# First chunk of a pre-LN attention and gMLP kernel: q's first four slices in two column halves, and an opening ordered by hand

## The chip, the cores and the metric

The kernel runs on one core of one Trainium2 chip. The metric is the device time in microseconds of one execution. A profile of one execution comes with the runs. TensorE is PE in the profile (its weight loads PEld), VectorE is DVE, ScalarE is ACT, GpSimd is POOL, and SP is the engine whose queue issues most DMAs.

## The reference

Input x has 2048 rows (tokens) of 1024 columns, in bfloat16. Two blocks follow each other, each behind a layer norm and each added to its input.

```python
x = A_x
h = x + _A_ref(_layernorm(x), A_wqkv, A_wo)
h2 = h + _B_ref(_layernorm(h), B_w_in, B_w_sp, B_b_sp, B_w_out)

# _A_ref: 32 heads of 32; a token looks at itself and at 7 earlier ones, 2 apart
qkv = (x @ wqkv).reshape(B, S, 3, H, Dh)              # wqkv: 1024 x 3072
logits = einsum('bhsd,bhswd->bhsw', q, kg) * scale    # kg: k at s, s-2, ..., s-14
o = einsum('bhsw,bhswd->bhsd', softmax(logits), vg)
return o.reshape(B, S, D) @ wo

# _B_ref: gated MLP with mixing over tokens
z = gelu(x @ w_in)                                    # w_in: 1024 x 3584
z1, z2 = z[..., :1792], layernorm(z[..., 1792:])
g = einsum('ts,bsf->btf', w_sp, z2) + b_sp[None, :, None]
return (z1 * g) @ w_out
```

## The kernel before

Tokens are cut into four chunks of 512 (`CH`), each of four tiles of 128. The matmuls that make q, k and v have a weight slice of 128 columns as the stationary operand (taken with a stride of 8 elements, so that a slice holds one eighth of every group of eight columns) and the transposed, normed tokens `xnT` of one chunk as the moving one, 512 columns wide. There are 8 slices (`dl`) for each of q, k and v, and 8 steps of contraction (`kt`) for each slice. Two slices share a PSUM accumulator of two banks (`new_acc`, three of them in the pool `ps_acc`; a second pool, `ps_att`, has one buffer with the tag `L`).

The kernel has three parts in time. The opening makes `xnT` of chunk 0: for each tile of 128 tokens statistics (`stats` on DVE, L222; `stats_act` on ACT for tile 3, L228), the reciprocal root (`rstd_of`, L237), the norm (`norm`, L242) and eight transposes on PE with a copy out of PSUM (`xpose`, L249). Behind it comes a long middle part, in which the closures of all stages (q, k, v, attention, output projection, the gMLP's first two products) are given to the planner `Order` (L61) with a duration, dependences and a priority each. `Order.run` simulates the engines from given starting clocks and calls the closures in the order of the planned starts; within this part each compute engine then works in exactly that order. Chunks 1 to 3 get their statistics through `ln1` (L290), with arrival times from `X_AT` (L287), go to DRAM normed (`xn_d`) and come back through a transposing DMA on SP's queue. Last comes a dense part: the mixing over tokens (L773) and the last product (L788).

In the opening before, the framework's own scheduler orders the engines' instructions; only `o_.run()` at L751 stands under a schedule kept by hand. q of chunk 0 is part of `qkv` (L329): its first four slices go kt by kt through two accumulators (L338 to L343), since wq arrives in eight pieces, one for each kt; the other slices go one after the other.

SP's queue issues, in this order: tiles 0 and 1 of x (ACT's queue issues 3 and 2), wq in eight pieces, wk, the four tiles of chunk 1, wv, the eight tiles of chunks 2 and 3. Two tiles of x share a buffer (`pairs`), and there are four such buffers, so the tiles of chunk 2 wait until the norms of chunk 0 have read theirs. Ahead of everything PE runs `NWARM` matmuls on zeros (L207).

Of the kernel before, what the change touches and what calls it, by code (L numbers as in the profile page):

```python
# [10 lines left out]
FP32 = mybir.dt.float32  # L11
BF16 = mybir.dt.bfloat16
# [19 lines left out]
NEG = -1.0e9  # L32
NWARM = 14
XRB = 2
# [90 lines left out]
def kernel(  # L125
# [17 lines left out]
    out2d = out[0]  # L143

    consts_d = nc.inline_tensor(_consts(), name="qt_consts")

# [14 lines left out]
    eps_t = cpool.tile([P, 1], FP32, name="eps_t")  # L161
    V.memset(eps_t[:], EPS)
    nhalf = cpool.tile([P, TPC], FP32, name="nhalf")
    V.memset(nhalf[:], -0.5)
    mv1 = cpool.tile([P, NT, 2], FP32, name="mv1")
# [12 lines left out]
    def new_acc():  # L178
        return ps_acc.tile([P, 2, CH], FP32, name="acc", tag="acc")
# [18 lines left out]

    def load_x(i):
        x_slot(i)  # L200
        dma(xts[i], x2d[i * P:(i + 1) * P, :])

# [3 lines left out]
    for _ in range(NWARM):  # L206
        T.matmul(wps[:], warm[:, 0:P], warm[:], start=True, stop=True)  # L207

    for i in (0, 3, 1, 2):
        x_slot(i)  # L210
        (dma if i < 2 else A.dma_start)(xts[i], x2d[i * P:(i + 1) * P, :])
    wsb = [wtile([P, KT, D], "wq", "wA"), wtile([P, KT, D], "wk", "wA"), wtile([P, KT, D], "wv", "wB")]
    for kt in range(KT):
        dma(wsb[0][:, kt, :], wq_view[:, kt, 0:D])
    dma(wsb[1][:], wq_view[:, :, D:2 * D])
    for i in range(TPC, 2 * TPC):
        load_x(i)
    dma(wsb[2][:], wq_view[:, :, 2 * D:3 * D])
    for i in range(2 * TPC, NT):
        load_x(i)  # L220

# [5 lines left out]

    def stats_act(i):  # L228
        sm = l1.tile([P, 4], FP32, name="sm", tag="sm")
        jk = l1.tile([P, D], BF16, name="jk", tag="xn", bufs=4)  # L230
        A.activation(jk[:], xts[i], ACTF.Identity, accum_out=sm[:, 0:1])
        A.activation(jk[:], xts[i], ACTF.Square, accum_out=sm[:, 1:2])
        V.tensor_scalar(mv1[:, i, 0:1], sm[:, 0:1], 1.0 / D, None, op0=ALU.mult)
        V.tensor_tensor(sm[:, 2:3], mv1[:, i, 0:1], mv1[:, i, 0:1], op=ALU.mult)
        V.scalar_tensor_tensor(mv1[:, i, 1:2], sm[:, 1:2], 1.0 / D, sm[:, 2:3], op0=ALU.mult, op1=ALU.subtract)

    def rstd_of(lo, hi):  # L237
        sd = l1.tile([P, TPC], FP32, name="sd1", tag="sd1")
        A.activation(sd[:, 0:hi - lo], mv1[:, lo:hi, 1], ACTF.Sqrt, bias=eps_t[:])
        V.reciprocal(rstd1[:, lo:hi], sd[:, 0:hi - lo])  # L240

# [7 lines left out]
    def xpose(i, xn):  # L249
        tp = ps_acc.tile([P, KT, P], BF16, name="tpa", tag="acc")  # L250
        for a in range(KT):
            T.transpose(tp[:, a, :], xn[:, a * P:(a + 1) * P], ident)  # L252
        (V.tensor_copy if i == 2 else A.copy)(xnT[0][:, :, i * P:(i + 1) * P], tp[:])

    wsq = l1.tile([P, 1], FP32, name="wsq", tag="wsq")
    A.activation(wsq[:], eps_t[:], ACTF.Sqrt)
    stats_act(3)
    stats(V, 0)
    rstd_of(0, 1)
    stats(V, 1)  # L260
    xpose(0, norm(0))
    rstd_of(1, 2)
    rstd_of(3, 4)
    xpose(1, norm(1))
    xpose(3, norm(3))
    stats(V, 2)
    rstd_of(2, 3)
    xpose(2, norm(2))
    wo_sb = wtile([P, DLO, D], "wo_sb", "wB")
# [8 lines left out]

    o_ = Order({"PE": 12.9, "ACT": 12.0, "DVE": 12.6, "POOL": 12.0}, {"acc": 3, "L": 1, "prod": 2, "part": 2, "xn": 4})
    add = o_.add  # L280
# [5 lines left out]

    X_AT = {1: 18.5, 2: 27.5, 3: 30.5}  # L287
    xn_ready = {}
# [25 lines left out]

    att_in = {}

    def alloc_att_in(c):
        qT = att.tile([P, DLO, CH], BF16, name="qT", tag="qT")
        kT = att.tile([P, DLO, HALO + CH], BF16, name="kT", tag="kT")
        vT = att.tile([P, DLO, HALO + CH], BF16, name="vT", tag="vT")  # L320
        att_in[c] = (qT, kT, vT)

    seq = [0]
# [5 lines left out]
    def qkv(c):  # L329
        for xi in range(3):  # L330
            wv = wsb[xi][:].rearrange("p kt (m dl) -> p kt dl m", dl=DLO)
            for dp in range(DLO // 2):
                key = ("acc", "qkv", c, xi, dp)
                deps = [G.get(("xnT", c))]
                if c == 0 and xi == 0 and dp < 2:
                    def mm(wv=wv, dp=dp):
                        if dp == 0:
                            accs = [new_acc(), new_acc()]  # L338
                            G["acc", "qkv", 0, 0, 0], G["acc", "qkv", 0, 0, 1] = accs
                            for kt in range(KT):  # L340
                                for dl in range(4):
                                    T.matmul(accs[dl // 2][:, dl % 2, :], wv[:, kt, dl, :], xnT[0][:, kt, :],  # L342
                                             start=(kt == 0), stop=(kt == KT - 1))  # L343
                    last = add("PE", 6.91 if dp == 0 else 0.0, mm, deps, prio=order(), take="acc")
                else:
                    for j in range(2):
                        def mm(j=j, dl=2 * dp + j, wv=wv, key=key):
                            if j == 0:
                                G[key] = new_acc()
                            for kt in range(KT):  # L350
                                T.matmul(G[key][:, j, :], wv[:, kt, dl, :], xnT[c][:, kt, :],  # L351
                                         start=(kt == 0), stop=(kt == KT - 1))
                        last = add("PE", 1.727, mm, deps, prio=order(), take="acc" if j == 0 else None)
                        deps = [last]
                def ev(xi=xi, dp=dp, key=key):
                    if c == 0:
                        off = 0 if xi == 0 else HALO
                        A.copy(att_in[0][xi][:, 2 * dp:2 * dp + 2, off:off + CH], G[key][:])  # L358
                        if xi > 0 and dp == 3:
                            dma(qkv_d[xi][:, :, CH - HALO:CH], att_in[0][xi][:, :, CH:CH + HALO])  # L360
                    else:
                        stg = l1.tile([P, 2, CH], BF16, name="stg", tag="xn", bufs=4)
                        A.copy(stg[:], G[key][:])  # L363
                        dma(qkv_d[xi][:, 2 * dp:2 * dp + 2, c * CH:(c + 1) * CH], stg[:])
# [9 lines left out]
    def attention(c):  # L374
        if c == 0:
            d_q = G["ev", 0, 0, 3]
            d_k, d_v = G["ev", 0, 1, 3], G["ev", 0, 2, 3]
# [318 lines left out]


    alloc_att_in(0)
    V.memset(att_in[0][1][:, :, 0:HALO], 0.0)
    V.memset(att_in[0][2][:, :, 0:HALO], 0.0)  # L700
    qkv(0)
# [47 lines left out]
    dma_op(0.0, wsp0, [G["z1ev", NCH - 2], G["close"]])  # L749
    with tc.manual_schedule(engines={mybir.EngineType.PE, mybir.EngineType.Activation, mybir.EngineType.DVE, mybir.EngineType.Pool}):  # L750
        o_.run()  # L751
    t2.close()
# [81 lines left out]
```

## Time and profile before

| what | value |
|---|---|
| median of 3 runs | 737.69 us (737.46 to 737.92) |
| time of the profiled execution | 737.65 us |
| its span | 735.9 us |
| mean granted clock of PE | 0.998 of full |
| PE busy | 725.7 us, 99% of the span |
| DVE, ACT, POOL busy | 416.8, 219.2, 50.0 us |
| DMA | 105.27 MB, mean 143 GB/s |

A line of a timeline gives the start in us, the busy time in us, engine, line of the code, operation, and written<-read tiles with shapes and the number of instructions merged into it; in brackets stands the time for which the engine was idle before it, and what ended that. A line of the windows gives the stretch in us, its length, the busy time of PE, PEld, DVE, ACT and POOL (with the number of instructions), the granted clock of PE as a share of full speed, the busy share of the DMA engines and GB/s. A matmul's listed duration (379 ns for 512 columns) is longer than its pitch, since matmuls are pipelined: 224 matmuls of L773 take 48.35 us in the chain, 0.216 us each.

### The profile page before, as it was taken

To read this page: it belongs to the slowest core of one execution; us is meant where nothing else is said; L and a number is where in the kernel's file an instruction comes from. 1 tells how busy PE (TensorE), PEld (TensorE's weight loads), DVE (VectorE), ACT (ScalarE), POOL (GpSimd) and SP (SyncE) were. 2 spreads that over 40 slices of the span, in tenths; PEclk is the share of its full clock that TensorE was granted. 3 is DMA by queue.
4 is the path that set the end of the run, shared out by engine and by line. 5 is a ranking of instruction groups with operands and counts; after the bars stand their busy time and mean duration, and the time that the engine had idled before them with its cause. 6 is when DMAs were issued, how large, how long until landed. Compare 5 with 4: busy or idle time off the path is not lost.

```text
span 735.9 us, 8608 instructions
## 1 busy us (share of the span) xinstructions
PE 725.7 (99%) x3580; PEld 369.1 (50%) x3580; DVE 416.8 (57%) x431; ACT 219.2 (30%) x267; POOL 50.0 (7%) x59
## 2 busy tenths in 40 slices
PE   7999999999999999999999999999999999999998
PEld 4666665566645444444444544444444444444444
DVE  4899899988999899889940012221232223212322
ACT  4322532534338954696563620000000000000000
POOL 0310200100102100300113000000000000000000
PEclk9999999999999999999999999999999999999999
DMA  9874563485484632370079988135104410020002
GB/s 337 315 242 116 191 184 122 153 231 200 149 324 109 210 113 74 115 227 18 29 229 338 256 243 268 40 95 148 58 29 112 133 57 31 28 86 29 1 15 71
DMA packets 113223, 105.27 MB, mean 143 GB/s; under 512 B 67776, under 2 KB 91744, under 8 KB 113056
## 3 DMA queue, kind: packets, MB, share of 16 engines
q1 hardware_dynamic: 105472, 72.63, 33.0%
q0 software_dynamic: 7280, 31.50, 12.1%
q8 instruction: 28, 0.46, 0.3%
q10 hardware_dynamic: 432, 0.59, 0.2%
q14 instruction: 11, 0.09, 0.0%
HBM read 55.09 MB, written 33.88 MB: 121 GB/s over the span
## 4 chain that ended last, share of the span: by engine, by line
PE 89%; DVE 7%; ACT 1%; POOL 1%; issue 1%; DMA 0%; POOLq 0%; DVEq 0%; ACTq 0%
PE acc L773 26%; PE acc L351 22%; PE acc L788 13%; PE acc L627 10%; PE acc L677 9%; PE acc L554 8%; DVE prod L504 2%; DVE oT L510 2%; PE acc L342 1%; DVE part L411 1%; POOL l3rstd L524 1%; PE L L430 1%; DMA xp<-in_A_x_dram 0%; PE tpa L252 0%; ACT z1s L683 0%
## 5 line engine op out<-in xcount | busy, mean ns | idle before, releaser
L773 PE MATMUL acc<-wspT,z2sb 128*128 128x512 bf16 x896 | 194.0, 379 | 0.0
L773 PEld LDWEIGHTS <-z2sb 128*128 128x128 bf16 x896 | 87.7, 98 | 105.7
L776 DVE TENSOR_TENSOR g<-acc,bB 128x1024 bf16<-128x1024 f32 x28 | 34.3, 1224 | 157.6 <-PE acc L773 133.0
L677 PE MATMUL acc<-hnT,win 128*128 128x512 bf16 x448 | 99.4, 379 | 0.5 <-ACT z1s L683 0.5
L627 PE MATMUL acc<-win,hnT 128*128 128x512 bf16 (+1 forms) x512 | 99.3, 352 | 0.0
L627 PEld LDWEIGHTS <-hnT 128*128 128x128 bf16 x512 | 49.8, 98 | 47.7 <-issue 0.9
L407 DVE TENSOR_TENSOR prod<-qT,kT 128x4096 bf16<-128x4096 bf16 x32 | 72.0, 2284 | 1.6 <-ACT kT L358 1.6
L788 PEld LDWEIGHTS <-zg 128*128 128x128 bf16 x462 | 45.2, 98 | 51.7
L677 PEld LDWEIGHTS <-win 128*128 128x128 bf16 x448 | 43.4, 98 | 52.5 <-issue 1.7
L504 DVE TENSOR_TENSOR prod<-vT,AB 128x4096 bf16<-128x4096 bf16 x28 | 63.8, 2289 | 1.0
L510 DVE TENSOR_TENSOR oT<-oT,prod 128x4096 bf16<-128x4096 bf16 x28 | 64.0, 2284 | 0.1
L363 ACT CAST stg<-acc 128x1024 bf16<-128x1024 f32 x36 | 36.4, 1011 | 78.6 <-PE acc L351 75.5
L788 PE MATMUL acc<-wout_a,zg 128*128 128x512 bf16 (+1 forms) x264 | 58.2, 373 | 0.0
L795 DVE TENSOR_TENSOR ot<-acc,hr 128x1024 bf16<-128x1024 f32 x15 | 18.4, 1224 | 69.4 <-PE acc L788 69.4
L351 PE MATMUL acc<-xnT,wv 128*128 128x512 bf16 x256 | 57.1, 380 | 0.0
L351 PE MATMUL acc<-xnT,wk 128*128 128x512 bf16 x256 | 57.1, 380 | 0.0
L554 PE MATMUL acc<-wo_sb,oT 128*128 128x512 bf16 x256 | 56.3, 379 | 0.7 <-DVE oT L510 0.7
L351 PE MATMUL acc<-xnT,wq 128*128 128x512 bf16 x224 | 49.8, 379 | 0.0
L351 PEld LDWEIGHTS <-wk 128*128 128x128 bf16 x256 | 36.4, 143 | 19.1 <-issue 0.9
L351 PEld LDWEIGHTS <-wv 128*128 128x128 bf16 x256 | 36.4, 143 | 19.1 <-issue 0.9
L788 PE MATMUL acc<-wout_b,zg 128*128 128x512 bf16 (+1 forms) x198 | 44.4, 373 | 0.0
L351 PEld LDWEIGHTS <-wq 128*128 128x128 bf16 x224 | 31.9, 143 | 16.8 <-issue 0.8
(125 smaller groups left out, 489.9 us busy)
## 6 DMA issues: line engine op xcount, KB each, us to landing
qkv_d<-stg SPq DMA_DIRECT2D x36, 256.0 KB, 2.5
z_d<-z1s SPq DMA_DIRECT2D x28, 256.0 KB, 2.6
z1c<-z_d SPq DMA_DIRECT2D x28, 256.0 KB, 2.7
z_d<-u SPq DMA_DIRECT2D x12, 448.0 KB, 2.9
z2sb<-z_d POOLq DMA_DIRECT2D x12, 448.0 KB, 9.2
xr<-in_A_x_dram SPq DMA_DIRECT2D x16, 256.0 KB, 2.8
h_d<-hb SPq DMA_DIRECT2D x16, 256.0 KB, 2.4
win<-in_B_w_in_dram POOLq DMA_DIRECT2D x2, 2048.0 KB, 9.1
```

The lines of the kernel that those rows point to most:

```text
L351: T.matmul(G[key][:, j, :], wv[:, kt, dl, :], xnT[c][:, kt, :], start=(kt == 0), stop=(kt == KT - 1))
L363: A.copy(stg[:], G[key][:])
L407: V.tensor_tensor(st["prod"][:], qT[:], kT[:, :, o:o + CH], op=ALU.mult)
L504: V.tensor_tensor(pvs[w][:], vT[:, :, o:o + CH], abb, op=ALU.mult)
L510: prev = add("DVE", 2.3, lambda w=w: V.tensor_tensor(oTs[c][:], oTs[c][:], pvs[w][:], op=ALU.add), [prev, m_], prio=3.0, lat=0.15, free="p ...
L554: T.matmul(st["acc", il][:, nh, :], oTs[c][:, dl, il * P:(il + 1) * P], wo_sb[:, dl, nh * CH:(nh + 1) * CH], start=(dl == 0), stop=(dl == ...
L627: T.matmul(accf[:, n0:n1], hnTs[c][:, il, kt, :], wins[hf][:, kt, n0:n1], start=(kt == 0), stop=(kt == KT - 1))
L677: T.matmul(G["accy", c, fp][:, j, :].rearrange("p (a b) -> p a b", a=TPC), wt[:, kt, f0 * P:(f0 + 1) * P], hnTs[c][:, :, kt, :], start=(kt ...
L773: T.matmul(acc[:, j, :], z2sb[a][:, f * P:(f + 1) * P], wspT[:, a, :], start=(a == 0), stop=(a == NT - 1))
L776: V.tensor_tensor(g1[:], acc[:], bB[:, c * CH:(c + 1) * CH].unsqueeze(1).to_broadcast([P, 2, CH]), op=ALU.add)
L788: T.matmul(outs, zg[:, f, il * P:(il + 1) * P], wt[:, f0, lo:hi], start=(f == 0), stop=(f == NF - 1))
L795: V.tensor_tensor(ot[:], acc[:].rearrange("p a b -> p (a b)"), hr[:], op=ALU.add)
```

## The change

The four compute engines are now ordered by hand from the start of the kernel. The opening is written out in the order that each engine shall keep:

- Tiles 0 and 1 of x are loaded in two halves of 64 partitions each, one on SP's and one on ACT's queue. Chunk 1's x (two loads of two tiles) goes ahead of wk, the first half of what follows ahead of wv.
- Two more matmuls on zeros; the constants' memsets go behind the one that these matmuls wait for.
- `stats_act` is split into two sums, and the second one and its variance come after tiles 0 and 1 have been transposed. Tiles 2 and 3 share one root.
- `xpose` puts its eight transposes into two PSUM banks of one buffer, even tiles in `L`, odd ones in `acc`; `xput` copies one half with ACT and the other with DVE.
- q's first four slices are made with 64 matmuls of 256 columns instead of 32 of 512: the left half, tokens of tiles 0 and 1, with `q_left`, between whose steps the transposes of tiles 2 and 3 stand; then the right half, slice by slice. The other four slices follow as before, all ahead of the planner, which gets later starting clocks and new arrival times.

```diff
-NWARM = 14
+NWARM = 16
...
+    by_hand = tc.manual_schedule(engines={mybir.EngineType.PE, mybir.EngineType.Activation, mybir.EngineType.DVE, mybir.EngineType.Pool})
+    by_hand.__enter__()
...
+    def load_pair(k):
+        x_slot(2 * k)
+        x_slot(2 * k + 1)
+        dma(pairs[k][:], x2d[2 * k * P:(2 * k + 2) * P, :].rearrange("(t p) d -> p t d", p=P))
...
-    for i in (0, 3, 1, 2):
-        x_slot(i)
-        (dma if i < 2 else A.dma_start)(xts[i], x2d[i * P:(i + 1) * P, :])
...
+    with tc.manual_schedule(engines={mybir.EngineType.SP}):
+        for i in range(TPC):
+            x_slot(i)
+        for i in range(2):
+            dma(xts[i][0:64], x2d[i * P:i * P + 64, :])
+            A.dma_start(xts[i][64:P], x2d[i * P + 64:(i + 1) * P, :])
+        dma(xts[2], x2d[2 * P:3 * P, :])
+        A.dma_start(xts[3], x2d[3 * P:4 * P, :])
+        for kt in range(KT):
+            dma(wsb[0][:, kt, :], wq_view[:, kt, 0:D])
+        load_pair(2)
+        load_pair(3)
+        dma(wsb[1][:], wq_view[:, :, D:2 * D])
+        load_pair(4)
+        load_pair(5)
+        dma(wsb[2][:], wq_view[:, :, 2 * D:3 * D])
+        load_pair(6)
+        load_pair(7)
...
     def xpose(i, xn):
-        tp = ps_acc.tile([P, KT, P], BF16, name="tpa", tag="acc")
+        tps[i] = ps_acc.tile([P, 2, 2 * CH], BF16, name="tpb", tag="acc") if i % 2 else ps_att.tile([P, 2, 2 * CH], BF16, name="tpa", tag="L")
         for a in range(KT):
-            T.transpose(tp[:, a, :], xn[:, a * P:(a + 1) * P], ident)
-        (V.tensor_copy if i == 2 else A.copy)(xnT[0][:, :, i * P:(i + 1) * P], tp[:])
+            T.transpose(tps[i][:, a // 4, (a % 4) * P:(a % 4 + 1) * P], xn[:, a * P:(a + 1) * P], ident)
+
+    def xput(i):
+        for hf, cp in ((0, A.copy), (1, V.tensor_copy)):
+            cp(xnT[0][:, 4 * hf:4 * hf + 4, i * P:(i + 1) * P], tps[i][:, hf, 0:CH].rearrange("p (a s) -> p a s", a=4))
+
+    def q_mm(dl, kt, lo, hi):
+        T.matmul(qacc[dl // 2][:, dl % 2, lo:hi], wqs[:, kt, dl, :], xnT[0][:, kt, lo:hi], start=(kt == 0), stop=(kt == KT - 1))
+
+    def q_left(lo, hi):
+        for kt in range(lo, hi):
+            for dl in range(4):
+                q_mm(dl, kt, 0, 256)
+
+    def q_out(dp):
+        A.copy(att_in[0][0][:, 2 * dp:2 * dp + 2, :], qacc[dp][:])
...
-    stats_act(3)
     stats(V, 0)
-    rstd_of(0, 1)
+    sd0 = root(0, 1)
+    sm = sums_act(3, 0)
     stats(V, 1)
-    xpose(0, norm(0))
-    rstd_of(1, 2)
-    rstd_of(3, 4)
-    xpose(1, norm(1))
-    xpose(3, norm(3))
+    sd1 = root(1, 2)
+    V.reciprocal(rstd1[:, 0:1], sd0[:, 0:1])
+    xn = {0: norm(0)}
+    V.reciprocal(rstd1[:, 1:2], sd1[:, 0:1])
+    xn[1] = norm(1)
+    xpose(0, xn[0])
+    xput(0)
+    xpose(1, xn[1])
+    xput(1)
+    qacc[0], qacc[1] = new_acc(), new_acc()
     stats(V, 2)
-    rstd_of(2, 3)
-    xpose(2, norm(2))
+    sums_act(3, 1, sm)
+    var_act(3, sm)
+    sd2 = root(2, 4)
+    V.reciprocal(rstd1[:, 2:4], sd2[:, 0:2])
+    xn[2], xn[3] = norm(2), norm(3)
+    q_left(0, 6)
+    xpose(2, xn[2])
+    xput(2)
+    q_left(6, 7)
+    xpose(3, xn[3])
+    xput(3)
+    q_left(7, KT)
+    for dp in range(2):
+        for dl in (2 * dp, 2 * dp + 1):
+            for kt in range(KT):
+                q_mm(dl, kt, 256, CH)
+        q_out(dp)
+    for dp in (2, 3):
+        qacc[dp] = new_acc()
+        for dl in (2 * dp, 2 * dp + 1):
+            for kt in range(KT):
+                q_mm(dl, kt, 0, CH)
+        q_out(dp)
...
-    o_ = Order({"PE": 12.9, "ACT": 12.0, "DVE": 12.6, "POOL": 12.0}, {"acc": 3, "L": 1, "prod": 2, "part": 2, "xn": 4})
+    o_ = Order({"PE": 24.8, "ACT": 25.8, "DVE": 14.4, "POOL": 12.0}, {"acc": 3, "L": 1, "prod": 2, "part": 2, "xn": 4})
...
-    X_AT = {1: 18.5, 2: 27.5, 3: 30.5}
+    X_AT = {1: 13.0, 2: 20.5, 3: 28.5}
```

In `qkv` the loop over q, k and v starts at k for chunk 0, and in `attention` the dependence of chunk 0 on q is a fixed planned time of 26.0.

## The prediction

> **What bounds the kernel now.** I read the page first: its engine row, the granted clock and the chain that ended last.
>
> ```profile
> span 735.9 us, 8608 instructions
> PE 725.7 (99%) x3580; PEld 369.1 (50%) x3580; DVE 416.8 (57%) x431; ACT 219.2 (30%) x267; POOL 50.0 (7%) x59
> PE 89%; DVE 7%; ACT 1%; POOL 1%; issue 1%; DMA 0%; POOLq 0%; DVEq 0%; ACTq 0%
> ```
>
> PE (TensorE) carries 89% of the chain. A 128x512 matmul takes its place every 0.216 us (the chain has 184 of L351 in 39.71 us), so a busy PE cannot go faster. What can be saved is PE's idle time, and there I read PE's timeline around the places where the chain leaves PE.
>
> ```profile
> 249.60 1.89 PE L677 MATMUL acc<-hnT,win 128*128 128x512 bf16 x8 [0.45 <-ACT z1s L683]
> 320.86 0.62 PE L430 MATMUL L<-part,csb 128*32 128x256 bf16 x16 [1.31 <-DVE part L411]
> 368.13 4.06 PE L554 MATMUL acc<-wo_sb,oT 128*128 128x512 bf16 x18 [0.74 <-DVE oT L510]
> ```
>
> These three waits, 0.45 + 1.31 + 0.74 = 2.5 us, are all the waiting shown from the first q matmul to the phase of L773, where PE runs dense to the end. The rest is the opening: q's first matmul starts at 13.32 us. So I read the opening's timeline.
>
> ```profile
> 4.42 0.69 DVE L224 BATCH_NORM_STATS2 bnst<-xp 128x6 f32<-128x512 bf16 x1 [3.07 <-DMA xp<-in_A_x_dram]
> 8.39 0.53 DVE L244 TENSOR_SCALAR xn<-xp,mv,rstd 128x1024 bf16<-128x1024 bf16 x1
> 8.98 3.46 PE L252 MATMUL tpa<-csb,xn 128*128 128x128 bf16 x32 [2.33 <-DVE xn L244]
> 12.48 0.69 DVE L253 COPY xnT<-tpa 128x1024 bf16<-128x1024 bf16 x1 [1.79 <-PE tpa L252]
> 13.32 7.10 PE L342 MATMUL acc<-xnT,wq 128*128 128x512 bf16 x32 [0.88 <-DVE xnT L253]
> 17.69 0.70 DVE L224 BATCH_NORM_STATS2 bnst<-xp 128x6 f32<-128x512 bf16 x1 [4.51 <-DMA xp<-in_A_x_dram]
> 27.17 3.19 PE L351 MATMUL acc<-xnT,wk 128*128 128x512 bf16 x14
> ```
>
> The way to 13.32 is: tile 0 of x lands, statistics, norm, 32 transposes, the last copy. Norm 0 ends at 8.92 although tile 0 landed at 4.4, because statistics of tiles 1 and 2 stand between. 27.17, k's first matmul, is my yardstick: q has the same 64 slices of 512 columns' work before and after. Last, the windows by microsecond, for the clock and the DMA.
>
> ```profile
> 8.00:9.00 1.00, 0.02 (x1) 0.02 (x2) 1.00 (x5) 0.44 (x2) 0.00 (x0) 1.00 1.06 389
> 9.00:10.00 1.00, 1.00 (x12) 0.98 (x12) 1.00 (x5) 0.37 (x2) 0.00 (x0) 0.58 1.06 389
> 11.00:12.00 1.00, 1.00 (x12) 1.00 (x11) 0.00 (x0) 1.00 (x2) 0.00 (x0) 0.50 1.06 389
> 12.00:13.00 1.00, 0.45 (x5) 0.18 (x2) 0.52 (x1) 0.77 (x1) 0.00 (x0) 0.71 1.04 383
> ```
>
> PE stood idle from 6.66 to 8.98; the clock fell to 0.50 near 9.2, and the transposes ran at 0.107 us each (3.46/32). It came back near 12.6. The warm-up matmuls changed from a pitch of 0.43 to 0.22 near 5.8. These three moments lie 3.4 us apart, so I take it that the clock is decided every 3.4 us from what PE did in the stretch before.
>
> **The change, part by part.**
>
> Loads. Today two tiles of 0.26 MB are in flight at once on SP and ACT, and the first lands at about 4.4. Halved across both queues, tile 0 has to share with nothing: at 399 GB/s (the row of 3 to 4 us) 0.26 MB is 0.66 us, so it lands up to 0.66 earlier. Bounds 3.75 and 4.4 (a half costs a whole one's latency); I take 3.8, as the queues start together. Tile 1 follows at 4.4 to 4.5, tile 3 at about 6.0 (1 MB and the 0.1 MB constants). ACT issues three DMAs instead of two, 0.45 us more, then the table load of 1.28: done by 3.6, hidden since ACT's first root comes at 5.4. wq is issued 0.45 us later on SP; the DMA share is full from 3 us on, so it lands by bytes all the same: 3.25 MB at 0.39 is 8.3 us, last slice near 11.1, slice 5 near 9.9, and PE needs slice 5 only after 11.
>
> To the first q matmul. Statistics of one tile take a pitch of 1.45 (17.69 to 19.14) and end 1.53 after their start (17.69 to 19.22). Tile 0: 3.8 to 5.33. Root on ACT (0.29): 5.7. ACT then sums tile 3 when it lands, 6.05 to 7.2 (1.16 from 4.60 to 5.76 in the old trace). This is an added wait: tile 1's root is queued behind it on ACT, 7.2 to 7.5, though its statistics are done at 6.8, and norm 1 waits for that root. DVE: reciprocal and norm 0 end at 7.43, norm 1 at 8.18. PE: transposes of tile 0 from 7.5. Eight took 0.94 to the copy at half clock (8.98 to 9.92); at full clock I take 0.65. Copies in halves, 1.02 on ACT and 0.69 on DVE for a whole tile, are about 0.6 and 0.4. Tile 1's transposes 8.25 to 8.9, its copy to 9.55. First q matmul: **9.65**, against 13.32. But it then has only half the columns, so most of these 3.7 us do not count.
>
> The second pair of tiles decides. DVE: statistics of tile 2 from 9.4 to 10.95. ACT: second sum of tile 3 9.55 to 10.8. Three small operations at pitches of 0.2 to 0.27: 11.6. Root 11.95, reciprocal 12.15, norms 2 and 3 end at 12.7 and 13.2. PE meanwhile does 24 left-half matmuls. Bounds for one: 0.109 (half of 0.216) if the weight load hides, 0.143 if the load is the pitch (the duration of a wq load under L351). I take 0.109: in the half-clock transposes loads of 0.152 lie one behind the other at 0.107, so a load's duration is not its pitch, and at the kernel's end 28 matmuls of 256 columns take 24.22 - 98 x 0.2158 = 3.07, or 0.110 each, under loads of 0.098. So 2.6 us, to 12.25. Transposes 2 12.75 to 13.4, four matmuls 0.44, transposes 3 from 13.75 to 14.35, copy to 15.0. Right half from **15.05**, 32 x 0.109 = 3.5, to 18.55; today these four slices end at 13.32 + 32 x 0.216 = 20.24. That is **1.7 us gained**; q's other four slices and k follow at an unchanged pitch, k at 25.45.
>
> Warm-up. Two more matmuls at 0.216 end at about 7.0: hidden, tile 0's transposes come at 7.5. If tile 0 landed any earlier than here they would still not be in the way.
>
> Clock. I assume full clock from 5.8 on. In the stretch 5.8 to 9.2 PE would be busy about 1.2 + 0.65 + 0.65 of 3.4 us, 73%; today it was 0.85 + 0.25, 32%, and the clock fell; the stretch after, 91% busy with transposes, brought it back. 73% is nearer to 91, but the threshold lies somewhere between. At half clock until 12.6, 14 left matmuls fit into 9.65 to 12.64, ten follow by 13.73, and the right half starts at 15.9: gain 0.8. The Trainium skill, "TensorE: Matmul & The Clock Gate", section on transposes in PE mode, says that these do not count as PE work for the clock. By it only the warm-up's 35% would count and the gain would be 0.8; this trace speaks against it, since the clock rose near 12.6 after nothing but transposes. The same page, section on packing small matmuls, says that a weight load overlaps a running matmul only in another row group. By it each half-column matmul would pay its load in full, 64 x 0.143 = 9.2 us; the 0.110 at the kernel's end disagrees.
>
> x of chunk 1 ahead of wk: 1 MB is 2.7 us more in front of wk, which lands near 11.1 + 2.7 + 5.4 = 19.2; PE needs it at 25.45: hidden. If that cover were gone it would cost at most the 2.7. SP then waits for norms 2 and 3 (13.2) before the second pair of chunk 2's x, with wv queued behind: wv lands near 27, needed at 25.45 + 13.8 = 39. DVE starts chunk 1's statistics near 15.1 instead of 17.69.
>
> The order after the opening is planned anew from other starting clocks. PE and DVE both come 1.7 earlier (attention waits for kT, which moves with PE). Chunk 3's norms, now inside chunk 0's attention (73.75 and after, 4 x 0.5), probably move before it: a lead of up to 2.0 us for DVE, which ends the waits of 1.31 and 0.74. Against it the new order can open waits. Bounds: 2.5 gained to some 4 lost; I take 0, since the plan past 40 us is much the same shifted.
>
> Sum: profiled execution 737.65 (span 735.9 and 1.75 around it) - 1.7 = **735.9**. The median, 737.69, is 0.04 above that execution.
>
> **The rivals.**
> 1. The waits behind go too: DVE's lead removes most of the 2.5 us. For it: two of the three waits end on DVE. Against: DVE waits for PE and ACT in attention, which eats a lead. 737.65 - 1.7 - 1.3 = about 734.6.
> 2. The clock stays at half through the left half: 737.65 - 0.8 = 736.8. For: 2.3 us of idle sufficed today. Against: the gaps shrink below 1 us.
> 3. Strided weight loads set the pitch at 0.143 on the halves: q_left's excess is 24 x 0.034 = 0.8, of which 0.5 lies in PE's wait for norm 2; four more cost 0.1; the right half 32 x 0.034 = 1.1. Gain 0.2: 737.4. For: 0.143 is longer than 0.109. Against: the overlapping loads named above.
> 4. Slower: the new order puts one more pair of exp and gelu table loads into the stretch near 242 to 250, where the chain runs on ACT (z1s 1.03, u 1.77, a table load of 1.28). Two loads and one eviction, 2 x 1.28 + 1.0 = 3.6, with nothing of PE's to cover them: 737.65 - 1.7 + 3.6 = 739.5. It decides once the added waits exceed 1.7; over 3.2 it is slower by 0.2%. For: PE already waits for z1s there. Against: relative distances after 40 us hardly change.
>
> **How the numbers follow.** 0.2% is 1.5 us, about what a measurement here can tell from no change. Forecast 0.50 (own range 735.2 to 736.7, for the unknown landing, transposes and small waits; four fifths of it beyond 0.2%), rival 1 0.15, rival 2 0.17, rival 3 0.06, rival 4 0.12. Faster 0.40 + 0.15 = 0.55; same 0.10 + 0.17 + 0.06 = 0.33; slower 0.12. The range from 734.2 to 737.8 takes in rivals 2 and 3 and most of rival 1; it leaves out rival 4 and the far end of rival 1.
>
> **What would show it.** Right: first statistics near 3.8, first q matmul at 9.4 to 10, left matmuls at a pitch near 0.11 and clock 1.00 throughout 6 to 16, right half near 15, k near 25.4, and waits of about 2.5 us in sum after that. Wrong: clock 0.50 in the 9 to 12.6 rows; a pitch near 0.14; k's first matmul waiting for a DMA; PE's idle before 442 us grown past 4 us, or k starting at 27 or later.

## The result, and the profile after

Five executions of the changed kernel have a median of **741.47 us** (740.09 to 741.65), against 737.67 for the kernel before beside them: a ratio of 1.0046, interval 1.0032 to 1.0061. The forecast of 735.9 us, faster, was wrong. By their mean granted clock, executions hold none, one or two stretches of 3.4 us at half clock (each takes 0.0023 off the mean): the kernel before, run here and beside the experiments, takes 736.7 to 737.2 us with none, 737.3 to 737.9 with one and 739.0 to 739.5 with two, and the two of the change's five that had none took 740.09 and 740.34. The profiled execution took 741.65 us. Its engine row and its chain by engine:

```profile
span 739.8 us, 8607 instructions
PE 723.1 (98%) x3553; PEld 370.7 (50%) x3614; DVE 419.1 (57%) x433; ACT 219.6 (30%) x267; POOL 50.1 (7%) x59
PE 86%; DVE 6%; DMA 5%; POOL 1%; issue 1%; ACT 0%; ACTq 0%; POOLq 0%; DVEq 0%
```

PE does the same products in a span that is 3.9 us longer. (The page lists 3614 weight loads, 34 more than before for the 32 halves and the two matmuls on zeros; of PE's own records some are missing.) DMA, 0% of the chain before, now has 5%. PE's timeline has the opening and the one large wait that is new:

```profile
8.15 0.62 PE L265 MATMUL tpa<-csb,xn 128*128 128x128 bf16 x8 [1.43 <-DVE xn L257]
9.61 0.62 PE L265 MATMUL tpb<-csb,xn 128*128 128x128 bf16 x8 [0.84 <-DVE xn L257]
10.90 2.78 PE L272 MATMUL acc<-xnT,wq 128*128 128x256 bf16 x24 [0.67 <-ACT xnT L269]
16.58 10.58 PE L272 MATMUL acc<-xnT,wq 128*128 128x256 bf16 x63 [0.23 <-ACT xnT L269]
27.00 13.33 PE L399 MATMUL acc<-xnT,wk 128*128 128x512 bf16 x60
63.05 1.03 PE L477 MATMUL L<-part,csb 128*32 128x512 bf16 x8 [3.08 <-DVE part L461]
```

k starts at 27.00 against 27.17: the opening gained 0.17 us, not 1.7. (The execution before had lost clock in its opening; where e5 below runs the same opening at full clock, k starts at 26.34.) What lost the time comes later, at 63.05, where attention's first `L` matmuls wait 3.08 us for DVE; before, that matmul ran at 60.07 without a wait:

```profile
60.07 0.62 PE L430 MATMUL L<-part,csb 128*32 128x512 bf16 x8
```

The windows of the change show that the wait is not its whole price:

```profile
63.00:64.00 1.00, 0.95 (x8) 0.12 (x7) 1.00 (x1) 0.00 (x0) 0.00 (x0) 0.56 0.00 0
65.00:66.00 1.00, 1.00 (x4) 0.38 (x3) 1.00 (x2) 0.00 (x0) 0.00 (x0) 0.50 0.00 0
66.00:67.00 1.00, 1.00 (x5) 0.46 (x4) 1.00 (x1) 0.00 (x0) 0.00 (x0) 0.74 0.00 0
```

The clock was halved behind the wait until about 66.5. The second group of `L` matmuls stands at 79.18 against 74.58, 4.60 later: 2.98 of it stood already at the first group, 1.62 came between. Later 0.85 comes back. The waits account for 0.51 of it: before they were 0.45, 1.31 and 0.74, now they are 1.67 and twice 0.16. The rest is not accounted for. L817 starts at 446.34 against 442.59. So -0.17 + 3.15 (from k to the first `L`) + 1.62 - 0.85 = **+3.75**.

DVE's timeline tells why the first `L` waits:

```profile
24.02 0.70 DVE L234 BATCH_NORM_STATS2 bnst<-xp 128x6 f32<-128x512 bf16 x1 [1.21 <-DMA xp<-in_A_x_dram]
33.54 0.69 DVE L234 BATCH_NORM_STATS2 bnst<-xp 128x6 f32<-128x512 bf16 x1 [1.79 <-DMA xp<-in_A_x_dram]
42.44 0.55 DVE L257 TENSOR_SCALAR xn<-xp,mv,rstd 128x1024 bf16<-128x1024 bf16 x1 [1.15 <-POOL rstd L366]
43.96 0.55 DVE L257 TENSOR_SCALAR xn<-xp,mv,rstd 128x1024 bf16<-128x1024 bf16 x1 [0.98 <-DMA xn_d<-xn]
45.92 0.55 DVE L257 TENSOR_SCALAR xn<-xp,mv,rstd 128x1024 bf16<-128x1024 bf16 x1 [1.41 <-DMA xn_d<-xn]
46.70 0.55 DVE L257 TENSOR_SCALAR xn<-xp,mv,rstd 128x1024 bf16<-128x1024 bf16 x1 [0.23 <-DMA xn_d<-xn]
47.16 4.49 DVE L454 TENSOR_TENSOR prod<-qT,kT 128x4096 bf16<-128x4096 bf16 x2
```

The planner put the four norms of chunk 3 (L257 at 42 to 47) ahead of chunk 0's attention (L454). Each needs an `xn` buffer, and the buffers are still being stored for chunk 2. Attention starts at 47.16 instead of 42.23, where before it waited for `kT` alone:

```profile
42.23 4.49 DVE L407 TENSOR_TENSOR prod<-qT,kT 128x4096 bf16<-128x4096 bf16 x2 [1.57 <-ACT kT L358]
```

From its start to the first `L` it is 15.85 us (47.16 to 63.0), so the old start left 60.07 - 58.1 = 2.0 us to spare; of 4.93 us of delay 2.9 show as PE's wait. Attention that starts by about 44 costs nothing. The upper two of DVE's lines in the change show where the chain comes from: the statistics of chunks 2 and 3, which stand ahead of the norms of chunks 1 and 2 on DVE, wait for x. The plan counted on 20.5 and 28.5 (`X_AT`); x landed at 24.0 and 33.5. The chain of waits goes back from the wait at 63 through four DMAs to tile 3 of x:

```profile
1.99 5.43 DMA xp<-in_A_x_dram
...
10.73 13.26 DMA xp<-in_A_x_dram
...
26.44 7.08 DMA xp<-in_A_x_dram
...
37.59 9.09 DMA xn_d<-xn
...
```

Last, the opening on DVE, where the missing 1.5 us lie:

```profile
4.02 0.69 DVE L234 BATCH_NORM_STATS2 bnst<-xp 128x6 f32<-128x512 bf16 x1 [2.71 <-DMA xp<-in_A_x_dram]
5.96 0.69 DVE L234 BATCH_NORM_STATS2 bnst<-xp 128x6 f32<-128x512 bf16 x1 [0.41 <-DMA xp<-in_A_x_dram]
9.01 0.55 DVE L257 TENSOR_SCALAR xn<-xp,mv,rstd 128x1024 bf16<-128x1024 bf16 x1
10.89 0.42 DVE L269 COPY xnT<-tpb 128x512 bf16<-128x512 bf16 x1 [1.00 <-ACT xnT L269]
11.23 0.68 DVE L234 BATCH_NORM_STATS2 bnst<-xp 128x6 f32<-128x512 bf16 x1
```

Tile 1 lands at 5.96, not 4.4 to 4.5. Tile 3 lands at 7.42, not 6.0, and its sum on ACT holds root 1, so that norm 1 starts at 9.01. The two halves of a copy do not run side by side: DVE's half waits for ACT's. And the statistics of tile 2 are queued behind that copy. The windows of before and after, at the same microsecond, show the loads:

```profile
4.00:5.00 1.00, 1.00 (x3) 0.30 (x2) 0.58 (x1) 0.40 (x1) 0.00 (x0) 1.00 1.06 410
```

```profile
4.00:5.00 1.00, 1.00 (x3) 0.30 (x2) 0.98 (x2) 0.12 (x1) 0.00 (x0) 1.00 0.98 227
```

The DMA engines are as busy, at 0.98, but move 227 GB/s instead of 410. From 2 to 8 us the rates of the windows add up to 1.77 MB after and 2.11 MB before. The 0.35 MB that are missing take 0.9 us at 0.39 MB in a microsecond.

### The profile page after: what moved, and what is told of

The parts are those of the page before. It is cut to its first block, busy times and chain, and to the rows that moved or that the text cites. A ratio compares the mean times of both kernels' runs of the same rounds, so it can differ in the third digit from the quotient of the medians.

```text
span 739.8 us, 8607 instructions
## 1 busy us (share of the span) xinstructions
PE 723.1 (98%) x3553; PEld 370.7 (50%) x3614; DVE 419.1 (57%) x433; ACT 219.6 (30%) x267; POOL 50.1 (7%) x59
## 4 chain that ended last, share of the span: by engine, by line
PE 86%; DVE 6%; DMA 5%; POOL 1%; issue 1%; ACT 0%; ACTq 0%; POOLq 0%; DVEq 0%
PE acc L817 26%; PE acc L399 16%; PE acc L832 13%; PE acc L724 12%; PE acc L674 10%; PE acc L601 7%; DMA xp<-in_A_x_dram 3%; DVE prod L454 3%; DMA xn_d<-xn 1%; DVE part L458 1%; PE L L477 1%; POOL l2rstd L571 1%; DVE prod L458 1%; POOL l3rstd L571 0%; DMA xr<-in_A_x_dram 0%
## 5 line engine op out<-in xcount | busy, mean ns | idle before, releaser
L817 PE MATMUL acc<-wspT,z2sb 128*128 128x512 bf16 x878 | 193.1, 379 | 0.9
L817 PEld LDWEIGHTS <-z2sb 128*128 128x128 bf16 x896 | 87.7, 98 | 105.7
L454 DVE TENSOR_TENSOR prod<-qT,kT 128x4096 bf16<-128x4096 bf16 x32 | 71.9, 2284 | 0.0
L399 PE MATMUL acc<-xnT,wq 128*128 128x512 bf16 x188 | 44.3, 388 | 0.2
L681 ACT ACTIVATE u<-acc 128x1024 bf16<-128x1024 f32 (+1 forms) x32 | 29.3, 916 | 36.1 <-PE acc L674 34.2
```

The source lines that it names most:

```text
L454: V.tensor_tensor(st["prod"][:], qT[:], kT[:, :, o:o + CH], op=ALU.mult)
L681: A.activation(st["u", il][:, hf * 1024:hf * 1024 + wd], G["accz", c, il, hf][:].rearrange("p a b -> p (a b)")[:, 0:wd], ACTF.Gelu_apprx_t ...
L817: T.matmul(acc[:, j, :], z2sb[a][:, f * P:(f + 1) * P], wspT[:, a, :], start=(a == 0), stop=(a == NT - 1))
```

## The experiments

Two questions stood open: what the norms ahead of attention cost, and what held the opening. The theory: the plan's place for chunk 3's norms costs the 3.8 us behind 42 us, and the halved loads and the serial copies cost the opening its 1.5. The rival: the loss is one thing, late data, and goes away with the loads alone.

The kernel before was run beside each of them; the ratios are to its executions there, and what share of these had lost clock differs a little.

**e1: the arrival times.** The change, with times for the planner that are later than x really is.

```diff
-    X_AT = {1: 13.0, 2: 20.5, 3: 28.5}
+    X_AT = {1: 15.0, 2: 24.2, 3: 33.8}
```

> The changed kernel with only the planned arrivals of x set to what its trace shows (X_AT 15.0, 24.2, 33.8 for chunks 1, 2, 3 instead of 13.0, 20.5, 28.5). DVE's order then has chunk 2's statistics behind chunk 1's norms, and chunk 3's norms behind the eight products of chunk 0's attention, as before the change. Theory A (chunk 3's norms stand ahead of attention on DVE and wait there for the buffers whose stores have not landed): attention starts near 42 us instead of 47.16, the first L matmuls do not wait 3.08 us, the clock stays at 1.00 from 60 to 70 us, and with k still starting at 27.0 the time is 737.0 to 737.8, 0.1 to 0.6 below the kernel before. Rival B (the opening itself or the new plan as a whole costs the time, the norms only show it): over 739.5.

Measured: 737.53 us (737.15 to 738.33, 12 executions), ratio 0.9994 (0.9984 to 1.0003). Its DVE timeline:

```profile
32.43 1.92 DVE L257 TENSOR_SCALAR xn<-xp,mv,rstd 128x1024 bf16<-128x1024 bf16 x4 [1.16 <-POOL rstd L366]
41.62 4.49 DVE L454 TENSOR_TENSOR prod<-qT,kT 128x4096 bf16<-128x4096 bf16 x2 [1.45 <-ACT kT L405]
```

Chunk 3's norms are no longer ahead of attention, which waits for `kT` again, as before the change. The first `L` doesn't wait. Three numbers take away 3.9 us, the whole loss against this mixture of executions. At equal clock the opening as changed is still the worse one: eleven of these twelve executions have a clock of 0.999 or 1.000 and take 737.15 to 737.82, the kernel before without half clock 736.7 to 737.2.

**e2: the order kept, the buffer wait removed.** Chunk 3's norms stay ahead of attention, but write over x in place of an `xn` buffer.

```diff
+            V.tensor_scalar(xts[i], xts[i], mv1[:, i, 0:1], rstd1[:, i:i + 1], op0=ALU.subtract, op1=ALU.mult)
...
-                xn = norm(i)
-                dma_w(xn_d[c][il * P:(il + 1) * P, :], xn[:])
+                xn = norm(i, inplace=(c == 3))
+                dma_w(xn_d[c][il * P:(il + 1) * P, :], xn if c == 3 else xn[:])
```

> The changed kernel with its order on every engine kept, but chunk 3's norms written in place over x, so that they wait for no buffer of xn. Theory A, if the wait for the stores is what costs: norms from 42.4 to 44.4, attention at about 44.5 instead of 47.16, the first L matmuls wait 0.4 us instead of 3.08, the clock stays full; time 737.5 to 738.5. Rival C (the norms' place alone costs, whatever they wait for): attention still 2.3 us later than the kernel before, time 739 to 740. Rival B: over 740.

Measured: 738.64 us (737.48 to 740.08), ratio 1.0009 (0.9998 to 1.002). The norms run from 41.52 to 43.4, attention starts at 43.35 and the first `L` doesn't wait. So in this execution the norms themselves fit in; it is the wait for the stores that didn't. The order kept is not free in all executions, though: the median stays 1.1 us above that of e1, and this profile doesn't show by what. The opening of this execution shows what the prediction had as a rival:

```profile
9.45 0.62 PE L268 MATMUL tpa<-csb,xn 128*128 128x128 bf16 x8 [2.81 <-DVE xn L260]
11.40 4.45 PE L275 MATMUL acc<-xnT,wq 128*128 128x256 bf16 x24 [0.67 <-ACT xnT L272]
```

Tile 1 landed at 7.25, PE stood for 2.81 us, and the 24 left-half matmuls took 4.45 us instead of 2.78, at a granted clock of 0.50 from 11.74 on. k started at 28.27.

**e3: root 1 ahead of tile 3's sum.** e1, with the added wait on ACT taken away by another order.

```diff
-    sm = sums_act(3, 0)
     stats(V, 1)
     sd1 = root(1, 2)
+    sm = sums_act(3, 0)
```

> As e1_arrivals, and on ACT the root of tile 1 ahead of the first sum of tile 3. In the changed kernel's trace tile 1's statistics ended at 7.49, its root started at 8.50, behind the sum that waited for tile 3 until 7.44. If this queueing is a part of the opening's missing 1.5 us: root at 7.55, norm 1 at about 8.2 instead of 9.01, first q matmul near 10.2 instead of 10.90, right half near 16.0 instead of 16.58, k near 26.4. If tiles 2 and 3 set the right half by themselves (second sum of tile 3 on ACT): k stays at 27.0 within 0.2.

Measured: 737.63 us (737.01 to 738.76), ratio 0.9997 (0.9986 to 1.0007). Norm 1 comes at 8.33 and k at 26.33, against 8.56 and 26.56 in e1. But these 0.23 us are not the wait: in e1's execution root 1 ended at 8.28, before norm 0 did (8.46), so that norm 1 waited for no root, and tile 1 landed 0.22 later than here (6.31 against 6.09). In the profile of the change, where tile 3 landed 1.46 behind tile 1, DVE waited 0.71 for root 1; these two executions don't tell what the other order is worth, and the times don't tell them apart.

**e4: whole loads.** e1, with tiles 0 to 3 loaded whole, as before the change.

```diff
-        for i in range(2):
-            dma(xts[i][0:64], x2d[i * P:i * P + 64, :])
-            A.dma_start(xts[i][64:P], x2d[i * P + 64:(i + 1) * P, :])
-        dma(xts[2], x2d[2 * P:3 * P, :])
-        A.dma_start(xts[3], x2d[3 * P:4 * P, :])
+        for i in (0, 3, 1, 2):
+            (dma if i < 2 else A.dma_start)(xts[i], x2d[i * P:(i + 1) * P, :])
```

> As e1_arrivals, with tiles 0 to 3 of x loaded whole, 0 and 1 on SP, 3 and 2 on ACT, as before the change. If the halved loads delay what comes behind (tile 1 landed at 5.96 and tile 3 at 7.44 with them): first statistics 0.4 later (4.42), but tile 1 by 5.6 and tile 3 by 4.6, root 1 at 7.4, norm 1 near 8.4, k near 26.4. If the halves help as meant: k later than 27.0 by 0.3.

Measured: 736.45 us (736.23 to 736.67), ratio 0.998 (0.9969 to 0.9991). The rate is that of before again:

```profile
4.00:5.00 1.00, 1.00 (x3) 0.30 (x2) 0.30 (x1) 0.00 (x0) 0.00 (x0) 1.00 1.05 408
```

Tile 0's statistics start later than with halves, at 4.70 against 4.02, and k still comes earlier, at 26.34. The time falls by 1.1 us against e1, more than k's 0.2 in the two profiles. All ten executions have a clock of 0.999 or 1.000, so a part of the ratio is clock that the kernel before loses in some of its executions; against those that lose none (736.7 to 737.2) e4 gains about 0.4.

**e5: the norms' place alone, in the kernel before.** No line of the opening is touched.

```diff
-    X_AT = {1: 18.5, 2: 27.5, 3: 30.5}
+    X_AT = {1: 16.0, 2: 21.5, 3: 26.0}
```

> The kernel before with only the planned arrivals of x made earlier (X_AT 16.0, 21.5, 26.0 instead of 18.5, 27.5, 30.5), so that DVE's order becomes that of the changed kernel: chunk 1's norms behind chunk 2's first statistics, all four norms of chunk 3 ahead of chunk 0's attention. Opening, loads and halves stay those of before. Theory A: attention starts at 45 to 48 us instead of 42.23, the first L matmuls wait 1 to 4 us, the clock falls in some executions, time 739 to 742. Rival B (the slowness belongs to the new opening): 737 to 738.2.

Measured: 743.15 us (741.7 to 745.28), ratio 1.0082 (1.0069 to 1.0095), more than the 739 to 742 expected. In its profile k starts at 26.34, but the norms wait for stores (one for 1.47), attention starts at 46.87 and the first `L` waits 3.45 us. By the 15.85 us found above, 46.87 would give 62.72; that `L` runs at 62.77. The place of the norms costs at least as much as in the change without any other part of it. The old opening ran at full clock here, and k's 26.34 is 0.66 earlier than with the changed opening.

**e6: the halved loads alone, in the kernel before.**

```diff
-        (dma if i < 2 else A.dma_start)(xts[i], x2d[i * P:(i + 1) * P, :])
+    for i in range(2):
+        dma(xts[i][0:64], x2d[i * P:i * P + 64, :])
+        A.dma_start(xts[i][64:P], x2d[i * P + 64:(i + 1) * P, :])
+    dma(xts[2], x2d[2 * P:3 * P, :])
+    A.dma_start(xts[3], x2d[3 * P:4 * P, :])
```

> The kernel before with only the loads of tiles 0 to 3 as in the change (tiles 0 and 1 in halves of 64 partitions on SP and ACT, 2 on SP, 3 on ACT). In the changed kernel's trace the DMA moved 227 to 352 GB/s from 3 to 8 us, where the kernel before moved 383 to 410. Theory D (halves of 64 partitions lower the rate): 227 to 350 GB/s in these rows here too, first statistics near 4.0 but tile 1 near 6, tile 3 near 7, and k 0.5 to 1.5 later than 27.17. Rival (the rate fell for the new order of what follows): 380 to 410 GB/s, k within 0.3 of 27.17.

Measured: 741.91 us (740.95 to 742.61), ratio 1.0061 (1.0048 to 1.0074). Its window and PE's timeline:

```profile
4.00:5.00 1.00, 1.00 (x3) 0.30 (x2) 0.99 (x2) 0.12 (x1) 0.00 (x0) 1.00 0.99 197
```

```profile
10.17 1.03 PE L256 MATMUL tpa<-csb,xn 128*128 128x128 bf16 x8 [3.02 <-DVE xn L248]
16.10 9.19 PE L346 MATMUL acc<-xnT,wq 128*128 128x512 bf16 x32 [0.88 <-DVE xnT L257]
```

Rates fall to 197 to 352 GB/s from 3 to 8 us, tile 2 lands at 8.25, the clock is at 0.50 from about 10.2 to 20.4, and q's first 32 matmuls take 9.19 us. k starts at 32.03. Here the loads alone undo more than the whole opening of the change could gain.

**e7: the copies side by side.** e4, with the halves of a tile's transposes in two PSUM tiles instead of two banks of one.

```diff
...
-            T.transpose(tps[i][:, a // 4, (a % 4) * P:(a % 4 + 1) * P], xn[:, a * P:(a + 1) * P], ident)
+            T.transpose(tps[i][a // 4][:, (a % 4) * P:(a % 4 + 1) * P], xn[:, a * P:(a + 1) * P], ident)
...
-            cp(xnT[0][:, 4 * hf:4 * hf + 4, i * P:(i + 1) * P], tps[i][:, hf, 0:CH].rearrange("p (a s) -> p a s", a=4))
+            cp(xnT[0][:, 4 * hf:4 * hf + 4, i * P:(i + 1) * P], tps[i][hf][:, 0:CH].rearrange("p (a s) -> p a s", a=4))
```

> As e4_whole, with the two halves of a tile's transposes in two PSUM tiles of their own, so that DVE's copy does not wait for ACT's. In e4_whole DVE's copy waits 0.68 and more for ACT's copy (tile 1: 9.60 to 10.18 on ACT, then 10.21 to 10.63 on DVE). If that chain is a part of the missing time: tile 2's statistics start 0.4 to 0.5 earlier (10.1 instead of 10.55), right half near 15.4 instead of 15.91, k near 25.9 instead of 26.34, time 736.0. If not: k at 26.3.

Measured: 735.74 us (735.57 to 735.82), ratio 0.9978 (0.9969 to 0.9987). DVE's copies no longer wait for ACT's (8.54 and 9.20), tile 2's statistics start at 9.54, and k comes at 25.24, 1.10 before e4. Of this, 0.40 is tile 0's landing, which varies between executions (first statistics at 4.30 here, at 4.70 in e4); the other 0.70 agrees with the medians, which are 0.71 apart. In the profile of the change DVE's copy is released by ACT's copy (1.00 us of idle); with two tiles it is released by PE (0.23). So the serial copies came with the shared tile: an order between two readers of it that no line of the kernel asks for.

**e8: the second pair first.** e4, with the order of the opening changed instead of the tiles: ACT's second sum of tile 3 and DVE's statistics of tile 2 go ahead of the first copies, and the transposes of tiles 2 and 3 come earlier among the left halves.

```diff
+    sums_act(3, 1, sm)
+    stats(V, 2)
+    var_act(3, sm)
...
-    stats(V, 2)
-    sums_act(3, 1, sm)
-    var_act(3, sm)
...
-    q_left(0, 6)
+    q_left(0, 4)
...
-    q_left(6, 7)
+    q_left(4, 6)
...
-    q_left(7, KT)
+    q_left(6, KT)
```

> As e4_whole, but the second pair's work comes earlier: ACT's second sum of tile 3 ahead of its copies, DVE's statistics of tile 2 and the variance of tile 3 ahead of DVE's copies, tiles 2 and 3 transposed after four and six of the eight steps of the left half. If the second pair's chain on DVE and ACT sets the right half, as the prediction put it: norms 2 and 3 from about 12.2, PE without waits of more than 0.3 from the first q matmul, right half near 15.0, k near 25.4, time 735.5 to 736.0, which would beat both kernels. If PE or the copies bind before: k at 26.0 to 26.3, time 736.2.

Measured: **735.39 us** (734.99 to 735.43), ratio 0.9973 (0.9962 to 0.9984): the best of all, faster than both kernels, and its slowest execution is 1.2 us below the fastest of the kernel before (736.68). PE's timeline has no wait behind the first q matmul:

```profile
10.03 1.91 PE L269 MATMUL acc<-xnT,wq 128*128 128x256 bf16 x16 [0.67 <-ACT xnT L266]
11.98 0.62 PE L262 MATMUL tpa<-csb,xn 128*128 128x128 bf16 x8
12.44 1.05 PE L269 MATMUL acc<-xnT,wq 128*128 128x256 bf16 x8
13.32 0.61 PE L262 MATMUL tpb<-csb,xn 128*128 128x128 bf16 x8
13.77 11.45 PE L269 MATMUL acc<-xnT,wq 128*128 128x256 bf16 x72
25.06 9.23 PE L396 MATMUL acc<-xnT,wk 128*128 128x512 bf16 x42
```

**e9: no column halves.** e8, with q's first four slices in 512 columns behind all four tiles.

```diff
-    q_left(0, 4)
...
+    for kt in range(KT):
+        for dl in range(4):
+            q_mm(dl, kt, 0, CH)
...
-                q_mm(dl, kt, 256, CH)
```

> As e8_early_second_pair, but q's first four slices in 32 matmuls of 512 columns after all four tiles, instead of two halves. If the column halves are worth what the prediction took (left-half matmuls fill PE's wait for the second pair at 0.109 each): tiles 2 and 3 transposed from 11.9, q from about 13.1, k at 13.1 + 13.85 = 27.0 instead of 25.06, time 737.2. If the halves bring nothing beyond the reordered opening: k at 25.1 to 25.5, time 735.5.

Measured: 739.42 us (739.05 to 740.73), ratio 1.0023 (1.0012 to 1.0034).

```profile
11.98 0.62 PE L262 MATMUL tpa<-csb,xn 128*128 128x128 bf16 x8 [2.63 <-DVE xn L254]
13.76 15.30 PE L269 MATMUL acc<-xnT,wq 128*128 128x512 bf16 x64 [0.70 <-ACT xnT L266]
```

The column halves are worth 4.0 us against e8: they fill the 2.63 us in which PE otherwise stands, and that keeps the clock up. Here 64 matmuls take 15.30 us instead of the 13.8 of full clock, and k comes at 28.89, later than the 27.0 expected: q starts 0.66 later than thought, and the half clock (13.06 to 16.47) had not been counted.

**e10: only the loads undone.** The change, with the edit of e4 and its own `X_AT`.

```diff
-            dma(xts[i][0:64], x2d[i * P:i * P + 64, :])
...
+            (dma if i < 2 else A.dma_start)(xts[i], x2d[i * P:(i + 1) * P, :])
```

> The changed kernel with only the loads of tiles 0 to 3 whole again; its planned arrivals, and so the norms of chunk 3 ahead of attention, stay. Theory A says that this is the smaller of the two faults: k near 26.3 instead of 27.00, DMA at 380 to 410 GB/s from 3 us, but attention still at 45 to 47 and the first L matmuls waiting 2 to 3.5 us; time 739.5 to 740.7. Theory D (the halved loads are the main fault, through the clock and everything that arrives late): 737 or below.

Measured: 738.54 us (737.08 to 740.11, 10 executions), ratio 1.0012 (1.0001 to 1.0024): between the two expectations. The profiled execution took 737.08, the lowest of the ten. Its DVE timeline:

```profile
40.97 2.23 DVE L254 TENSOR_SCALAR xn<-xp,mv,rstd 128x1024 bf16<-128x1024 bf16 x4 [1.15 <-POOL rstd L363]
43.12 4.47 DVE L451 TENSOR_TENSOR prod<-qT,kT 128x4096 bf16<-128x4096 bf16 x2
```

The norms stand ahead of attention as in the change, but none waits for a store, and attention at 43.12 is in time for the first `L`; the second group of `L` waits 1.10 us for DVE. Chunk 3's x is issued at 24.63 instead of 26.44 and chunk 2's norms come 1.5 us earlier. Their stores take 6.5 us to land (median of the four issues from 35 to 39 us) instead of 8.1, beside the transposing DMA that brings chunk 1 back. This run and e4 differ in nothing but `X_AT`, and their medians are 2.1 us apart; with the halved loads (the change and e1) it is 3.9. So the norms' place costs time by itself, as in e5, and the late loads add to what it costs. What the slower of the ten executions waited for no profile shows. Why the stores themselves took 1.6 us longer was not settled.

**e11: halves of columns.** e8, with tiles 0 and 1 loaded in two halves that keep all 128 partitions.

```diff
-        for i in (0, 3, 1, 2):
-            (dma if i < 2 else A.dma_start)(xts[i], x2d[i * P:(i + 1) * P, :])
+        for i in range(2):
+            dma(xts[i][:, 0:CH], x2d[i * P:(i + 1) * P, 0:CH])
+            A.dma_start(xts[i][:, CH:D], x2d[i * P:(i + 1) * P, CH:D])
+        dma(xts[2], x2d[2 * P:3 * P, :])
+        A.dma_start(xts[3], x2d[3 * P:4 * P, :])
```

> As e8_early_second_pair, but tiles 0 and 1 loaded in two halves again, one on SP and one on ACT: halves by columns (128 partitions, 512 columns each) instead of by partitions. If the loss of rate comes from halves that cover 64 partitions only: 380 to 410 GB/s from 3 us, tile 0 at 3.9 to 4.1, tile 1 by 5.3, k at 24.7 to 25.1, time 735.0 to 735.4. If it comes from more and smaller DMAs in flight at the start, whatever they cover: 230 to 350 GB/s again, tile 1 near 6, k later than 25.5, time over 736.

Measured: 738.63 us (736.37 to 739.95, 10 executions), ratio 1.0001 (0.9987 to 1.0014), 3.2 us above e8. The profile is of an execution of 739.71:

```profile
4.00:5.00 1.00, 1.00 (x3) 0.30 (x2) 0.96 (x4) 0.03 (x1) 0.00 (x0) 1.00 0.75 195
```

```profile
10.01 1.04 PE L265 MATMUL tpb<-csb,xn 128*128 128x128 bf16 x8 [1.90 <-DVE xn L257]
11.72 3.57 PE L272 MATMUL acc<-xnT,wq 128*128 128x256 bf16 x16 [0.67 <-ACT xnT L269]
```

Tile 0 lands earliest of all, its statistics start at 3.41. But the rate dips to 195 GB/s all the same, tile 3 lands near 7.8, root 1 and norm 1 (9.41) wait for its sum, and at PE's gap of 1.90 us the clock halves: 16 matmuls take 3.57 us. So the dip is not a matter of 64 partitions alone. That it comes with splitting is shown; which property of it costs is open, since here the engines were busy for 0.75, not 0.98. The clock is not all of it either: the four executions at 0.999 and 1.000 took 736.37 to 736.68, still 1.0 to 1.3 above e8.

## Why the prediction was wrong, step by step

**Right.** Full clock from 5.8 to beyond 16 and no half clock in the left halves: 1.00 in every window. That was partly luck. The stretches of 3.41 us lay elsewhere than in the trace before: from 5.09 to 8.50 and on to 11.91, with PE busy for 1.99 and 1.90 us, 58% and 56%, not the 73% worked out for 5.8 to 9.2. e2 and e11 lost the clock behind stretches with 1.58 and 1.51. The pitch of a half-column matmul: 24 in 2.78 us, the 0.109 that was taken; rival 3 is out. Eight transposes in 0.62 (0.65 taken). The second pair of tiles decides, and from the right half to k it is 10.42 us (10.40 predicted). x of chunk 1 ahead of wk is hidden, k waits for no DMA. Tile 0 at 4.02 lies within its bounds. Two of the three old waits went, as rival 1 had it for a gain, but the third grew from 1.31 to 1.67.

**Wrong, the sum's largest term: the new plan, taken as 0 between 2.5 gained and 4 lost.** It cost 3.75 + 0.17 = 3.9 us, next to the bad end. This is the step that failed. The prediction saw that chunk 3's norms would move ahead of attention and read that as a lead for DVE. The move was right; its sign was not. Two things were not asked of it: which buffer the moved norm needs (an `xn` that chunk 2's stores still held) and how much attention could be delayed before `L` waits (2.0 us). e1 gives the term back by three numbers, e2 and e10 give most of it back by two ways to shorten the wait, and e5 shows it in the old kernel. The 1.6 us of half clock behind the wait was no part of any bound. The 1.7 us of gain, too, were counted from a 27.17 that contains half clock; without it, in e5, the old opening reaches k at 26.34.

**Wrong: the loads land "by bytes all the same".** Tile 1 came 1.5 us late and tile 3 1.4. The rate of 399 GB/s was read from whole loads and used for halved ones; e4 and e6 show 408 and 197 in the same microsecond. This step also fed the other one: x of chunks 2 and 3 came later than the plan's 20.5 and 28.5. The prediction's own landings (wk 19.2, wv near 27, and 1.3 us for the 0.52 MB behind each) would have agreed with the plan, so the plan and the prediction shared the error. Halving is only a part of it: with whole loads, in e10, the statistics still start at 22.21 and 32.07. Chunk 3's x also waits for buffers that the norms of chunk 1 free (issued at 26.44, landed 7.08 later), and counting bytes leaves that out.

**Wrong: copies in halves in parallel.** They are serial, and tile 2's statistics queued behind them. Tile 2's statistics at 11.23 instead of 9.4 moved the second pair to 13.79 and the right half from 15.05 to 16.58. In steps of k, parallel copies are worth 0.7 (e4 to e7, without the difference in landing) and whole loads 0.2 to 0.8 (e1 to e4, change to e10); together they are 0.9 to 1.5 of the 1.55 us by which k missed its 25.45. With whole loads, e7 starts k at 25.24 and e8 at 25.06, where the prediction had it.

**The rivals.** The change was slower, but not by rival 4: no table loads were added near 242. It was rival 4's mechanism in another place, an added wait over 1.7 us that nothing of PE's covers. Two of the conditions for being wrong were met: waits past 4 us before the dense phase (3.08 + 1.67) and k at 27.0.

## What to carry to other kernels

When a planner is given new numbers, hold each planned arrival against the landing in the trace, and for each step that moves ahead of another ask which buffer it needs, who holds it, and how much slack its followers have. When a transfer is split in order to land earlier, take its rate from a row with split transfers. Two engines that read halves of one tile run side by side only where the program lets them; look for a wait of one on the other.

## What the runs showed of the hardware

**A split start of loads moves less per busy microsecond.** On ACT's queue (q10), in the microsecond from 4 to 5, before:

```profile
q10 hardware_dynamic: 103, 0.21, 53.1%
```

and after:

```profile
q10 hardware_dynamic: 75, 0.14, 64.7%
```

The columns are packets, MB and the share of 16 engines: 0.531 x 16 / 103 = 0.08 us for a packet before and 0.138 after, for rows of 2 KB in both. In e11 the same queue took 0.09 (23 packets, 13.0%): there the engines were less busy, and the packets hardly slower. The Trainium skill, "Perfetto Trace Analysis", section on DMA optimizations, says that splitting may help where the DMA engines are mostly idle. That agrees with the loss here, where they were 0.95 to 1.06 busy from 3 to 10 us; that splitting slows the packets themselves it doesn't say.

**The length of PE's gap does not decide the clock.** A gap of 1.90 us halved it in e11 and one of 2.33 in the kernel before, but e5, with 3.01 us idle at about the same place, ran its transposes at full clock:

```profile
8.98 2.38 PE L252 MATMUL tpa<-csb,xn 128*128 128x128 bf16 x32 [3.01 <-DVE xn L244]
```

What decides, by the traces here, is how a gap falls into stretches of 3.41 us. Where they begin shows in each trace, as the moment at which the warm-up's pitch falls from 0.43 to 0.22 us: 5.75 in the kernel before, 5.09 in the change, 4.37 in e5, 4.92 in e2 and 6.54 in e11, although the warm-up starts at 1.2 in all of them. (The clock's column has 1.00 ahead of that moment too; the trace has no record of the clock there.) Every later change of the clock lies whole stretches behind: the change lost it at 63.11, 17 x 3.413 after 5.09, and e5 at 62.40, 17 x 3.413 after 4.37. Three such stretches, in the kernel before, in e2 and in e5:

```profile
5.75:9.16 3.41, 1.08 (x7) 0.38 (x6) 3.41 (x15) 1.82 (x6) 0.00 (x0) 1.00 1.06 389
8.33:11.74 3.41, 1.58 (x20) 1.34 (x21) 2.39 (x9) 2.35 (x6) 0.00 (x0) 1.00 1.06 390
4.37:7.78 3.41, 1.60 (x8) 0.49 (x5) 3.41 (x11) 2.39 (x5) 0.00 (x0) 1.00 1.05 395
```

PE was busy for 1.08 and 1.58 us in the first two, and the next stretch ran at 0.50; it was busy for 1.60 in the third, and the clock stayed at 1.00. No stretch of any run here, up to the dense phase, lost the clock with more than 1.6 us or kept it with less: in these runs the limit lies near 47% of PE's listed busy time. The 3.01 us of e5 were shared by two stretches, the 2.33 of the kernel before lay in one.

The Trainium skill, "TensorE: Matmul & The Clock Gate", section on what is actually happening, has a window of 3.4 us that runs freely, whatever the kernel does. The 17 whole stretches and the different beginnings agree with that. From its advice, in the section on why this matters, no gaps over about 3 us, these rows differ: 1.90 sufficed.
